# Token-major values in four column groups, and keys, queries and values of a pair's two head groups kept apart

## The chip, the cores and the metric

The kernel runs on one core of one Trainium2 chip. The metric is the device time of one execution in microseconds (us); lower is better. Engines are named as in the profile: PE is TensorE (matmuls; PEld its weight loads), DVE is VectorE, ACT is ScalarE, POOL is GpSimd, SP is SyncE, whose queue issues most DMA transfers.

## The reference, cut to what matters

The model has four layers, A, B, A, B, each with a residual around a LayerNorm. A is attention with a recurrent memory over 64 segments of 32 tokens; B is a mixer and an MLP over all 2048 tokens. All tensors are bf16, the width is 640, and A has 32 heads of 192.

```python
def _A_ref(x, mem0, Wq, Wk, Wv, Wo, seg_len):   # M = 8 memory rows, seg = 32
    mem = mem0
    for s in range(n_seg):
        h = jnp.concatenate([mem, x[:, s * seg:(s + 1) * seg]], axis=1)   # 40 rows
        q = jnp.einsum('btd,dhe->bhte', h, Wq)
        k = jnp.einsum('btd,dhe->bhte', h, Wk)
        v = jnp.einsum('btd,dhe->bhte', h, Wv)
        scores = jnp.where(mask, jnp.einsum('bhqe,bhke->bhqk', q, k) * scale, -1e9)
        o = jnp.einsum('bhqk,bhke->bhqe', _softmax(scores), v)
        o = jnp.einsum('bhte,hed->btd', o, Wo)
        mem = o[:, :M]
        outs.append(o[:, M:])

def _B_ref(x, w1, w2, w3, w4):
    h = _gelu(_layernorm(x) @ w1)
    # four quarters of h are shifted along the tokens by +1, -1, +2, -2
    x1 = x + shifted(h) @ w2
    return x1 + _gelu(_layernorm(x1) @ w3) @ w4
```

## The kernel before

Both attention layers run at once, as two lanes. Step `t` works on segment `t` of the first attention layer (lane 0) and on segment `t - 5` of the second (lane 1), so 69 steps do all the attention; steps 5 to 63 have both lanes, 80 rows (`NS`) in all, and the ten at the two ends have one lane, 40 rows (`L1`). Every second step a chunk of 64 tokens of each lane goes through layer B between the attention's matmuls.

The 32 heads are eight groups of four (`HG`), 768 weight columns each, and two groups make a pair; a step has four pairs. For each pair `proj_pair` (from L552) records the projections of both groups, and `attend` (from L658) records the rest of each group:

- Keys and queries (L577): 30 matmuls a group, 6 column blocks of 128 by 5 chunks of the contraction. The weight block is the stationary side and `hT`, the transposed rows, streams (80 columns; 56 in a one-lane step). The result, in PSUM as `psk` or `psq`, is copied to `kT` by three VectorE copies (L595, L601) and to `qT` by one ScalarE copy (L587).
- Values in a two-lane step: the same 30 matmuls into `psv`, a ScalarE copy to `vF` (L607), six transposes on TensorE into `pvt` (L615) and two copies to `V`, rows as tokens (L624 VectorE, L626 ScalarE).
- Values in a one-lane step (`values`, L630 on): the rows are the stationary side and 384 weight columns stream. The two groups of the pair lie in two column groups of 64 of the array (L641), so the result is token-major at once and is copied to `V` directly (L652, L654).
- `attend`: scores into `pss` (L670), minimum and mask on VectorE (L681), exponent to `Pm` on ScalarE (L688), sum, reciprocal and product on VectorE (L692 to L694), a transpose into `pst` (L703), a copy to `PT` (L708), the product with `V` into `pso` (L717), two copies to `oT` (L727, L729), and the output projection into `psy` (L744), which is shared by the whole step and whose first rows are the memory of the next step (L768 copies them to `hT`).

There is one `kT`, one `qT` and one `V`. `proj_pair` records both groups' projections first and then `attend` twice. So the copies of the second group land in the same tiles before the first group's scores and product read them: both groups of a pair compute with the keys, queries and values of the second.

The order on every engine is written by a planner (`Plan`). Each operation is added with an engine, an estimated duration and a due time. `place` then lays all operations out in time, on each engine taking among those that could start soonest the one with the earliest due time, and the kernel is written in that order. PSUM banks (six for attention, class A; two for layer B) and slots of the weight ring are given out in the course of it. Due times come from `AT` (shares of a pair's 12 us at which k, q and v are due) and `AT_J` (the same for the second group of the pair).

Weights do not all fit on the chip. Of each pair's key, query and value weights, some of the five chunks stay resident and the others (`STREAM`, `MORE`), 384 KB each, are loaded anew in every step by SP (L475) into a ring of nine slots (`RING_A`); layer B has a ring of three (L513). A slot is freed by the last matmul that reads it. A chunk holds the columns of both groups of the pair.

Of the kernel before, what the change touches and what calls it, by code (L numbers as in the profile page):

```python
# [27 lines left out]
V_ONE = (0, 1, 2, 3)  # L28
V_ON = ("DVE", "ACT")
KEEP = True  # L30
WO_FROM = 1
AT = (0.0, 0.2, 0.5)
AT_J = 0.1
# [6 lines left out]
OT_BUFS = 8  # L40
KT_BUFS = 1
VT_BUFS = 1
HALVES = tuple(range(8))
ONE = 56
WARM = (2, 4, 2, 1, 1, 1, 1, 6, 1, 1, 2, 1, 1)
LAT = 0.12
# [25 lines left out]
class Slotted(Buf):  # L72


    __slots__ = ("cls", "make", "slot", "left", "free_at", "obj")

    def __init__(self, cls, make):
        super().__init__()
        self.cls = cls
        self.make = make  # L80
        self.slot = None
        self.left = 0
        self.free_at = 0.0
        self.obj = None


class Op:
    __slots__ = ("e", "d", "due", "fn", "n", "succ", "ready", "slots", "start", "end", "dma", "i", "margin",
                 "paced", "last", "after")


class Plan:
# [8 lines left out]
    def add(self, e, d, due, fn, r=(), w=(), a=(), dma=0, queue=None, margin=0.0, after=()):  # L101
        op = Op()
        op.e, op.d, op.due, op.fn, op.dma, op.margin = e, d, due, fn, dma, margin
# [5 lines left out]
        preds = set(after)  # L109
# [31 lines left out]
    def place(self):  # L141
# [24 lines left out]
        srv = 0.0  # L166
        out = []

        def est(o, t):
            s = max(t, o.ready)  # L170
            need = {}
            for b in o.slots:
                if b.slot is None:
                    need[b.cls] = need.get(b.cls, 0) + 1
            for c, n in need.items():
                fs = self.free_slots[c]
                if len(fs) < n:
                    return None
                s = max(s, fs[n - 1][0])
# [14 lines left out]
        while left:  # L194
            best = None
            for e in engines:
# [17 lines left out]
                s, o = min((so for so in vals if so[0] <= lim), key=lambda so: (so[1].due, so[1].i))  # L214
# [9 lines left out]
            o.end = s + o.d  # L224
            free[e] = o.end
# [36 lines left out]
def kernel(  # L262
# [102 lines left out]
    vFw = ctile([P, GC * NS], bf16, "vF")  # L365
    vF = vFw[:].rearrange("p (c n) -> p c n", c=GC)
# [31 lines left out]
    nc.vector.memset(vFw[:], 0.0)  # L398
# [24 lines left out]
    def ps(cls, shape, dtype, name):  # L423
        b = Slotted(cls, None)

# [97 lines left out]
    kept = {}  # L523

# [11 lines left out]
    def attention_step(t):  # L536
# [17 lines left out]
        def proj_pair(i_, pr):  # L554
            s0 = base + sl * 2 * i_
            for kind, at in zip("kqv", AT):
                if i_ == 0 and t > 0 and KEEP:
                    wbs, wv = kept[kind]
                else:
                    wbs, wv = load_pair(kind, pr, s0 + at * 2 * sl, LEAD_A)  # L560
                if i_ == NPAIR - 1:
                    kept[kind] = wbs, wv
                if kind == "v" and not both and i_ in V_ONE:
                    values(i_, pr, s0 + at * 2 * sl, wbs, wv)
                    continue
                for j in range(2):
                    G = t * NG + 2 * i_ + j
                    due = s0 + (at + AT_J * j) * 2 * sl
                    pq = ps("A", [P, GC, NS], f32, "ps" + kind)

                    nres = KC - STREAM[kind] + MORE.get((kind, pr), 0)
                    for kcs in [range(0, nres)] + [range(kc, kc + 1) for kc in range(nres, KC)]:
                        def fn(op, pq=pq, wv=wv, j=j, kcs=kcs):
                            o = T(pq)
                            for cc in range(GC):
                                for kc in kcs:
                                    nc.tensor.matmul(out=o[:, cc, 0:W],  # L577
                                                     lhsT=wv(kc, GW * j + cc * P, GW * j + (cc + 1) * P),
                                                     rhs=h[:, kc, cw:cw + W], start=(kc == 0 and cc == 0),
                                                     stop=(kc == KC - 1), skip_group_check=True)  # L580
                        wb = wbs[0] if kcs[0] == 0 else wbs[1 + kcs[0] - nres]
                        add("PE", mm_us(W, k=GC * len(kcs)), due + 0.01 * kcs[0], fn, r=(wb, *hk), a=(pq,))
                    if kind == "q":
                        q = qT

                        def fq(op, pq=pq, q=q):
                            nc.scalar.copy(out=q[:, :, c0:c0 + N], in_=T(pq)[:, :, off:off + N])  # L587
                        add("ACT", act_us(GC * N), due, fq, r=(pq,), w=(B("qT"),))
                    elif kind == "k":
                        k_ = kT[G % KT_BUFS]  # L590

                        def fk(op, pq=pq, k_=k_):
                            p4 = T(pq)[:].rearrange("p (h c) n -> p h c n", h=2)
                            k4 = k_[:].rearrange("p (h c) n -> p h c n", h=2)
                            nc.vector.tensor_copy(out=k4[:, :, 0::3, c0:c0 + N], in_=p4[:, :, 0::2, off:off + N])  # L595
                        add("DVE", dve_us(4 * N), due, fk, r=(pq,), w=(B("kT", G % KT_BUFS, 0),))
                        for part, (r0, r1, jj) in enumerate(((0, 64, 1), (64, P, 2))):
                            def fk2(op, pq=pq, k_=k_, r0=r0, r1=r1, jj=jj):
                                p4 = T(pq)[:].rearrange("p (h c) n -> p h c n", h=2)
# [766 lines left out]
```

## Time and profile before

| | us |
|---|---|
| median of 3 runs | 3415.71 (3415.09 to 3416.42) |
| profiled execution, span from the first to the last instruction | 3411.3 |
| 0 to 90: the first step, weights arriving | PE busy 54 of 90 |
| 90 to 300: the other one-lane steps at the start | PE busy 194 of 210 |
| 300 to 3150: two-lane steps | PE busy 2817 of 2850 |
| 3150 to 3380: the one-lane steps at the end | PE busy 207 of 230 |
| 3380 to 3411: the last chunk of layer B | PE busy 20 of 31 |

The profile is of one execution; its span leaves out what lies before the first and after the last instruction. A busy TensorE is not one at its peak, since the ends of matmuls are modelled and their lengths overlap; how long a matmul occupies the engine is read from the distance of starts. The costliest groups that belong to the values, from the page (line, engine, operation, tiles, shape, count | busy us, mean ns | idle before, and what ended it):

```profile
L626 ACT COPY V<-pvt 80x384 bf16<-80x384 bf16 x472 | 224.2, 475 | 186.4 <-PE pvt L615 170.3
L607 ACT CAST vF<-psv 128x480 bf16<-128x480 f32 x472 | 262.2, 556 | 71.7 <-PE psv L577 66.7
```

### The profile page before, as it was taken

What the parts mean: (1) busy time and instruction counts of PE and PEld (TensorE: products, weight loads), DVE (VectorE), ACT (ScalarE), POOL (GpSimd) and SP (SyncE); (2) the same over time, 40 slices, a digit from 0 to 9 for tenths busy, and PEclk for the clock granted to TensorE, in tenths of its full rate; (3) what the DMA queues carried; (4) which work ended last, traced back from release to release, by engine and by line L of the source; (5) the groups of instructions that cost most, each with busy time, mean ns of one, the idle gap of its engine ahead of it and who ended that gap; (6) DMA issues with size and microseconds to landing.
All of it is one profiled execution on the core that took longest, in us unless ns stands there. A gap on an engine that the chain in (4) does not pass through costs nothing.

```text
span 3411.3 us, 183231 instructions
## 1 busy us (share of the span) xinstructions
PE 3293.4 (97%) x82493; PEld 3163.7 (93%) x82493; DVE 2395.2 (70%) x7360; ACT 1681.5 (49%) x4045; POOL 237.2 (7%) x488
## 2 busy tenths in 40 slices
PE   5989999999999999999999999999999999999987
PEld 4779999999999999999999999999999999999776
DVE  3667777777777777777667777767777777777665
ACT  1345545455555555555455555555555555555433
POOL 1000000000000000000000000000000000000000
PEclk7999999999999999999999999999999999999999
DMA  9777667766766776677668667766776676677775
GB/s 373 250 271 266 234 221 254 246 221 230 262 237 226 242 269 220 222 253 252 222 225 276 226 221 240 259 226 224 267 242 220 227 266 237 226 245 263 255 268 199
DMA packets 409739, 834.28 MB, mean 245 GB/s; under 512 B 39632, under 2 KB 207263, under 8 KB 408952
## 3 DMA queue, kind: packets, MB, share of 16 engines
q1 hardware_dynamic: 401656, 809.47, 69.3%
q8 instruction: 645, 10.57, 1.2%
q0 software_dynamic: 7136, 13.00, 1.1%
q14 instruction: 142, 1.16, 0.1%
q10 hardware_dynamic: 160, 0.08, 0.0%
HBM read 817.14 MB, written 5.24 MB: 241 GB/s over the span
## 4 chain that ended last, share of the span: by engine, by line
PE 91%; DMA 4%; issue 2%; DVE 1%; ACT 1%; SPq 1%; POOL 0%; POOLq 0%; ACTq 0%; DVEq 0%
PE psy L744 16%; PE psq L577 16%; PE psk L577 16%; PE psv L577 15%; PE pvt L615 5%; PE pso L717 4%; PE pss L670 4%; PE psh L1160 3%; PE y L1205 3%; PE pst L703 2%; PE psv L641 1%; PE psh L1038 1%; PE hs L1097 1%; DMA wst<-in_A_Wq_dram 1%; DMA wst<-in_A_Wv_dram 1%
## 5 line engine op out<-in xcount | busy, mean ns | idle before, releaser
L577 PEld LDWEIGHTS <-wst 128*128 128x128 bf16 x24468 | 994.5, 99 | 32.8 <-issue 18.0
L744 PE MATMUL psy<-oT,wo 128*128 128x80 bf16 (+1 forms) x16560 | 664.0, 200 | 14.1 <-DMA wo<-in_A_Wo_dram 7.4
L744 PEld LDWEIGHTS <-wo 128*128 128x128 bf16 x16560 | 616.0, 100 | 19.9 <-issue 10.3
L587 ACT CAST qT<-psq 128x480 bf16<-128x480 f32 (+1 forms) x552 | 292.2, 529 | 333.7 <-PE psq L577 323.9
L729 DVE CAST oT<-pso 128x240 bf16<-128x240 f32 (+1 forms) x552 | 214.5, 389 | 339.1 <-ACT oT L727 322.2
L577 PE MATMUL psk<-hT,wst 128*128 128x80 bf16 (+1 forms) x9108 | 430.1, 200 | 4.4 <-DMA wst<-in_A_Wk_dram 2.2
L577 PE MATMUL psq<-hT,wst 128*128 128x80 bf16 (+1 forms) x8280 | 401.1, 200 | 10.7 <-issue 6.5
L577 PE MATMUL psq<-hT,wq 128*128 128x80 bf16 (+1 forms) x8280 | 377.6, 200 | 14.6 <-DVE V L624 5.9
L688 ACT ACTIVATE Pm<-pss,sm 80x320 bf16<-80x320 f32 (+2 forms) x552 | 279.9, 507 | 200.4 <-DVE sm L681 200.2
L727 ACT CAST oT<-pso 128x240 bf16<-128x240 f32 (+1 forms) x552 | 190.2, 345 | 368.1 <-PE pso L717 343.6
L577 PE MATMUL psk<-hT,wk 128*128 128x80 bf16 (+1 forms) x7452 | 349.7, 200 | 16.9 <-ACT hT L768 10.8
L577 PE MATMUL psv<-hT,wst 128*128 128x80 bf16 x7080 | 348.3, 202 | 5.9 <-issue 5.5
L577 PEld LDWEIGHTS <-wq 128*128 128x128 bf16 x8280 | 328.0, 99 | 21.2 <-issue 14.3
L601 DVE CAST kT<-psk 64x160 bf16<-64x160 f32 (+1 forms) x1104 | 336.0, 304 | 14.6
L577 PE MATMUL psv<-hT,wv 128*128 128x80 bf16 x7080 | 332.7, 202 | 1.1 <-issue 0.8
L577 PEld LDWEIGHTS <-wk 128*128 128x128 bf16 x7452 | 299.5, 100 | 30.7 <-issue 29.2
L708 ACT COPY PT<-pst 80x320 bf16<-80x320 bf16 (+1 forms) x552 | 222.7, 403 | 209.1 <-PE pst L703 204.5
L626 ACT COPY V<-pvt 80x384 bf16<-80x384 bf16 x472 | 224.2, 475 | 186.4 <-PE pvt L615 170.3
L681 DVE CUSTOM_DVE_ANT_1 pss<-pss,mask 80x320 f32<-80x320 f32 (+2 forms) x552 | 251.7, 476 | 82.0 <-PE pss L670 79.0
L595 DVE CAST kT<-psk 128x320 bf16<-128x320 f32 (+1 forms) x552 | 254.8, 462 | 62.5 <-PE psk L577 55.0
L607 ACT CAST vF<-psv 128x480 bf16<-128x480 f32 x472 | 262.2, 556 | 71.7 <-PE psv L577 66.7
L577 PEld LDWEIGHTS <-wv 128*128 128x128 bf16 x7080 | 291.0, 100 | 6.1 <-issue 1.5
(146 smaller groups left out, 4646.0 us busy)
## 6 DMA issues: line engine op xcount, KB each, us to landing
wst<-in_A_Wk_dram SPq DMA_DIRECT2D x555, 384.0 KB, 5.2
wst<-in_A_Wq_dram SPq DMA_DIRECT2D x486, 384.0 KB, 5.2
wst<-in_A_Wv_dram SPq DMA_DIRECT2D x486, 384.0 KB, 5.3
wstB<-in_B_w_dram SPq DMA_DIRECT2D x495, 320.0 KB, 4.7
wstB<-in_B_w_dram SPq DMA_DIRECT2D x132, 160.0 KB, 4.6
wo<-in_A_Wo_dram SPq DMA_DIRECT2D x8, 960.0 KB, 12.5
xw<-in_A_x_dram POOLq DMA_DIRECT2D x31, 80.0 KB, 5.0
x2d<-vbg POOLq DMA_DIRECT2D x31, 80.0 KB, 5.0
```

The source lines that it names most:

```text
L577: nc.tensor.matmul(out=o[:, cc, 0:W], lhsT=wv(kc, GW * j + cc * P, GW * j + (cc + 1) * P), rhs=h[:, kc, cw:cw + W], start=(kc == 0 and cc ...
L587: nc.scalar.copy(out=q[:, :, c0:c0 + N], in_=T(pq)[:, :, off:off + N])
L595: nc.vector.tensor_copy(out=k4[:, :, 0::3, c0:c0 + N], in_=p4[:, :, 0::2, off:off + N])
L601: nc.vector.tensor_copy(out=k4[r0:r1, :, jj, c0:c0 + N], in_=p4[r0:r1, :, 1, off:off + N])
L607: nc.scalar.copy(out=vF[:, :, c0:c0 + N], in_=T(pq)[:, :, off:off + N])
L626: nc.scalar.copy(out=dst, in_=src)
L681: nc.vector.tensor_tensor_reduce(out=o, in0=o, in1=maskt.unsqueeze(1).to_broadcast([NR, HG, N]), scale=-scale, scalar=3.0e38, op0=ALU.add, ...
L688: nc.scalar.activation(out=Pb[0:NR, :, 0:N], in_=o, func=ACT.Exp, bias=sm_[0:NR, 0:1], scale=-1.0)
L708: nc.scalar.copy(out=Pt[:, :, 0:N], in_=T(pst)[0:NS, :, c0:c0 + N])
L727: nc.scalar.copy(out=o_[:, 3:6, off:off + N], in_=T(pso)[:, 3:6, 0:N])
L729: nc.vector.tensor_copy(out=o_[:, 0:3, off:off + N], in_=T(pso)[:, 0:3, 0:N])
L744: nc.tensor.matmul(out=o[:, m, cw:cw + W], lhsT=wo[:, cc, m * P:(m + 1) * P], rhs=o_[:, cc, 0:W], start=st, stop=True, skip_group_check=True)
```

## The change

1. `proj_pair` is split. `loads` gets the weights of a pair, `keys_queries` records the keys and queries of one group, and the values of both groups are recorded together. The recorded order of a pair is now: loads, keys and queries of the first group, values of both, `attend` of the first, keys and queries of the second, `attend` of the second. So the second group's copies to `kT` and `qT` wait until the first group's scores have read them. `V` has two tiles, one for each group of the pair.
2. In two-lane steps a new function, `values3`, replaces the value matmuls, the copy to `vF` and the transposes. The 80 rows are the stationary side, in three column groups of 32, 32 and 16; the fourth column group carries a quarter of the pair's columns for one of the three row parts. Three PSUM banks take 15 rounds of four matmuls of 384 columns, and six copies bring them to `V`.
3. The planner learns of the array's modes (`mode`, a price `SWITCH` for a change, and a preference to stay in a mode), of order edges (`order`) that add no wait of their own, and of banks kept free (`keep`: an operation of the keys or queries takes a bank only if two others stay free).
4. `AT`, `AT_J`, `OT_BUFS` and `VT_BUFS` change, and one LayerNorm step of layer B is recorded a little later.

```diff
-V_ONE = (0, 1, 2, 3)
-V_ON = ("DVE", "ACT")
+V_ONE = ("DVE", "ACT")
+V_ON = ("ACT", "DVE", "ACT", "ACT", "ACT", "DVE")
-AT = (0.0, 0.2, 0.5)
-AT_J = 0.1
+AT = (0.0, 0.1, 0.5)
+AT_J = 0.25
+KEEP_KQ = 2
-OT_BUFS = 8
+OT_BUFS = 7
-VT_BUFS = 1
+VT_BUFS = 2
+SWITCH = 0.095
...
-        preds = set(after)
+        preds = {*after, *order}
...
             for c, (k, n) in need.items():
                 fs = self.free_slots[c]
-                if len(fs) < n:
+                if len(fs) < n + k:
                     return None
...
-                s, o = min((so for so in vals if so[0] <= lim), key=lambda so: (so[1].due, so[1].i))
+                stay = e == "PE" and mode
+                s, o = min((so for so in vals if so[0] <= lim),
+                           key=lambda so: (so[1].mode != mode if stay else False, so[1].due, so[1].i))
...
-    vFw = ctile([P, GC * NS], bf16, "vF")
-    nc.vector.memset(vFw[:], 0.0)
...
+        def values3(i_, pr, s0, wbs, wv):
+            banks = [ps("A", [P, GWH], f32, "psv") for _ in range(3)]
+            for r in range(3):
+                def fv(op, r=r):
+                    o = T(banks[r])
+                    for kc in range(KC):
+                        for u in range(4):
+                            g3, b = (u, r) if u < 3 else (r, 3)
+                            n3 = min(32, NS - 32 * g3)
+                            a = GWH * b
+                            nc.tensor.matmul(out=o[32 * u:32 * u + n3, :], lhsT=h[:, kc, 32 * g3:32 * g3 + n3],
+                                             rhs=wv(kc, a, a + GWH), start=(kc == 0), stop=(kc == KC - 1))
+                add("PE", mm_us(GWH, k=KC), s0 if r == 0 else s0 - STEP + 0.01 * r, fv, r=(*wbs, *hk),
+                    w=tuple(banks) if r == 0 else (), a=(banks[r],) if r else (), mode=32, order=placed_before("pso") if r == 0 else ())
+            for r in range(3):
+                v_copy(V_ON[r], s0, banks[r], (0, NS), (r // 2, r % 2, 0, NS), B("V", r // 2, r % 2, 0))
+                n3 = min(32, NS - 32 * r)
+                v_copy(V_ON[3 + r], s0 + 0.1, banks[r], (96, 96 + n3), (1, 1, 32 * r, 32 * r + n3), B("V", 1, 1, r))
...
-            add("PE", mm_us(N, N, 4) + mm_us(2 * N, N, 2), hi - HI[0], fs,
-                r=(B("qT"), B("kT", G % KT_BUFS, 0), B("kT", G % KT_BUFS, 1), B("kT", G % KT_BUFS, 2)), w=(pss,))
+            last_op["pss"] = add("PE", mm_us(N, N, 4) + mm_us(2 * N, N, 2), hi - HI[0], fs,
+                order=placed_before("pst"), r=(B("qT"), B("kT", G % KT_BUFS, 0), B("kT", G % KT_BUFS, 1), B("kT", G % KT_BUFS, 2)), w=(pss,))
...
-            proj_pair(i_, pr)
+            got = loads(i_, pr)
+            keys_queries(i_, pr, 0, got)
+            (values3 if both else values)(i_, pr, base + sl * 2 * i_ + AT[2] * 2 * sl, *got["v"])
             attend(2 * i_, 2 * pr)
+            keys_queries(i_, pr, 1, got)
             attend(2 * i_ + 1, 2 * pr + 1)
```

`v_copy` copies one bank's rows to one `V` tile, on the engine that `V_ON` (two lanes) or `V_ONE` (one lane) names. `pst` has an order edge after the last `pso`, like that of `pss` after the last `pst`. The matmuls of `keys_queries`, of `values` and of `attend` are those of before.

## The prediction

> **What bounds the kernel now.** I read the page's engine line, the chain that ended last, the idle time in windows, TensorE's timeline in two places, then the waits of SP's DMA queue and the DMA issues.
>
> ```profile
> span 3411.3 us, 183231 instructions
> ...
> PE 3293.4 (97%) x82493; PEld 3163.7 (93%) x82493; DVE 2395.2 (70%) x7360; ACT 1681.5 (49%) x4045; POOL 237.2 (7%) x488
> ...
> PE 91%; DMA 4%; issue 2%; DVE 1%; ACT 1%; SPq 1%; POOL 0%; POOLq 0%; ACTq 0%; DVEq 0%
> ```
> ```profile
> 2000.00:3150.00 1150.00, 1138.95 (x28569) 1115.81 (x28566) 832.13 (x2494) 598.07 (x1397) 77.61 (x157) 1.00 0.71 241
> 3150.00:3380.00 230.00, 207.11 (x5545) 176.75 (x5542) 152.71 (x547) 92.97 (x268) 17.07 (x35) 0.99 0.76 265
> ```
>
> TensorE is the bound: 97% busy, 91% of the chain, and in the two-lane steps (the first window) idle for 11 of 1150 us. So a TensorE instruction saved there is time saved. The one-lane steps at the end are looser: 207 of 230 us.
>
> A two-lane step pays for a pair's values so (start, length, engine, line, tiles, count):
>
> ```profile
> 1002.77 0.60 PE L577 MATMUL psv<-hT,wv 128*128 128x80 bf16 x12
> 1003.20 0.81 PE L577 MATMUL psv<-hT,wst 128*128 128x80 bf16 x18
> 1003.85 0.73 PE L670 MATMUL pss<-kT,qT 128*128 128x80 bf16 x12
> 1004.42 0.59 PE L577 MATMUL psv<-hT,wv 128*128 128x80 bf16 x12
> 1004.85 0.50 PE L615 MATMUL pvt<-ident,vF 128*128 128x128 bf16 x6
> 1005.18 0.81 PE L577 MATMUL psv<-hT,wst 128*128 128x80 bf16 x18
> ```
>
> Lengths overlap, so take starts: the 30 matmuls of one group run from 1002.77 to 1003.85, 36 ns each; six transposes from 1004.85 to 1005.18, 56 ns each. The new form has one relative in the trace, the one-lane L641, which uses two column groups of 64:
>
> ```profile
> 3204.82 0.54 PE L670 MATMUL pss<-kT,qT 128*128 128x40 bf16 x12
> 3205.30 0.51 PE L641 MATMUL psv<-wv,hT 128*40 128x384 bf16 x4
> 3205.64 0.65 PE L641 MATMUL psv<-wst,hT 128*40 128x384 bf16 x6
> 3206.22 0.37 PE L717 MATMUL pso<-PT,V 80*128 80x40 bf16 x8
> ```
>
> Ten matmuls of 384 columns take 3205.30 to 3206.22, 0.92 us. Their single records start 3 ns apart in twos, and the twos 163 ns apart: both column groups stream at once, and a round costs one stream of 384 columns (the 128-column transpose at 56 ns gives 0.42 ns a column, 160 ns, and 3 over). Entering the mode costs 80 ns (the first start follows its forerunner by 109 to 130 ns where 25 to 40 is usual), leaving it 95 ns (258 where 163 is usual).
>
> **The change, part by part.**
>
> *Values in 59 two-lane steps, 4 pairs each, 236 pairs.* Removed per pair: 60 x 36 ns + 12 x 56 ns = 2.832 us. Added: 60 matmuls in four column groups of 32, 15 rounds of four. If four groups share a round as two do: 15 x 163 + 80 + 95 = 2.620 us; in the new order all 60 stand together, so one entry and one exit. Saved 0.212 us x 236 = **50.0 us**. Bounds of the round: 163 ns, if the 3 ns are a price of each stream; 170 ns, if each further group adds 3.3 ns (15 x 236 x 7 = 25 us less saved); 326 ns, if the groups went two by two. I take 163, the row itself; the last is a rival.
>
> A rule speaks against it. The Trainium skill, "TensorE: Matmul & The Clock Gate", Part 3 (what overlaps and what doesn't), lets a weight load overlap a running matmul only where the row group differs; column groups share all rows. The trace disagrees for two groups: L641's weight loads last 95 to 100 ns, start within 3 ns of the matmuls that run, and the round is still 163. By the rule each of the 3540 rounds would be some 100 ns longer, an estimate of 354 us more.
>
> *One-lane steps.* The two value blocks of a pair now stand together: the new order enters the 64-column mode 40 times instead of 72. 32 x 175 ns = **5.6 us** saved.
>
> *Copies.* Per pair ScalarE had 2 x (556 + 475) ns and gets 4 x 475 = 1.90 us; VectorE had 2 x 350 and gets 2 x 552 (L652, the same 384 f32 columns), 94 us more in all: 2395 becomes 2490, under 75%. Hidden under TensorE's 97%. Without that cover it would be the 0.4 us a pair.
>
> *Waits among the engines.* Each TensorE wait has a cover: the TensorE work, priced at its rows, that stands between the instruction that starts a chain and the one that waits for its end. I counted covers in both built orders and compared them with what the chains take in this trace. Gone: the waits of psq for V's copies (L624) and of pvt for vF, 11.4 and 3.2 us in the steady part by the starts of the records. New: the second group's keys and queries may be copied to kT and qT only after the first group's scores. Queued behind such a waiting copy are VectorE's softmax and ScalarE's exponents, and the chain's next link, pst, waits for these. Scores to pst need 3.0 us (2.76 from the trace, 0.2 for the last matmul's end and the release); a tenth of the new covers is under 3.10, and the sum short is 2.5 us (before 1.7). pst over PT to pso needs 0.73 us (0.51 likewise); the tenth falls from 0.86 to 0.71, and 7.1 us are short where none were. oT and qT: 5.3 us, before 1.9. Where the two old waits stood, pst and pso are what is late next. So 11 us more by count, 15 less: **0**, with -15 and +25 as ends (the kept wait for hT at each step's head, some 20 us, stays).
>
> *Weight chunks.* The nine-slot ring is the tight place, as SP's queue shows (whom it waited for, us in all, times, longest; then one kind of chunk with its median us from issue to landing):
>
> ```profile
> SPq L475 <- PE psk L577: 747.9, 288, 17.6
> SPq L475 <- PE psv L577: 225.2, 219, 3.7
> ```
> ```profile
> wst<-in_A_Wk_dram SPq DMA_DIRECT2D x555, 384.0 KB, 5.2
> ```
>
> SP issues a chunk when PE has freed its slot. A key or query chunk serves both groups of a pair, and the second group's matmuls now come after the first's scores, so the slot is freed later. From the freeing matmul to the first use of the new chunk, two-lane steps, the cover falls from a median of 9.6 us to 8.1, its least value from 6.0 to 3.8. Needed, from the freeing matmul's issue to landing: a median of 5.15 us, 5.65 in the worst quarter. Short of 5.15: 6.5 us in the two-lane part, 9.2 and 4.9 in the first and last one-lane steps, before 0.2 in all: **+20**. Ends: 0 (a late chunk's wait lengthens its neighbours' cover) and +74 (short of 5.65: 53.8 + 15.4 + 13.0, before 8.3).
>
> *The rest.* A vF memset goes and one for a second V comes: under the first step's loads, under 1 us if bare. One LayerNorm step of the MLP is recorded later, 0.45 us on VectorE: order alone. The order edges issue nothing. Of the moved second group, 60 matmuls, three kT copies and one qT copy, all are counted above; its loads aren't moved, since a pair's chunks are still loaded at once, but q's fall due 1.2 us earlier in SP's queue (0.1 for 0.2 of 12 us), ahead of the MLP's chunks; POOL's queue is not passed. Seven oT for eight: a step's eighth group takes the first's, whose psy stands early. All **0**.
>
> Sum: 3411.3 - 50.0 - 5.6 + 0 + 20 = 3376 us of span. The median of the runs shown, 3415.7, is 4.4 us above the profiled span; with these **3380 us**.
>
> **The rivals.** (A) *The ring decides.* Place: L475's issues behind psk and psq. Price +74 instead of +20: 3434 us. It decides from landings of about 5.5 us, where the shortfall eats the 55.6 us saved. For it: 69% DMA busy already, bursts of three chunks, SP's 748 us behind psk. Against: a median landing leaves 20. (B) *Four column groups don't share a round.* Each ns of a round costs 3.54 us, so from 10 ns more (35 us) the change loses; two by two, 3380 + 577 = 3957 us. For it: no row has four. Against: two cost what one does. The skill's same part lists 2.38x for three column groups; by that ratio, an estimate, a round would be some 26% longer, 150 us in all. (C) *The ring costs nothing*, because waits overlap: 3360 us, and 3345 if also the 15 us of removed waits come without new ones. (D) *Nothing measurable*: the saved 55.6 us go into short covers, as (A) at 49 to 63 us of its price. That the change doesn't do what it says is excluded for the order (per group psk, psq, pss; 14160 matmuls of 32 columns), so this is no case.
>
> **How the numbers follow.** My forecast, 3362 to 3408: 0.48. (C), under 3362: 0.18. (D), within 0.2% (7 us, about what a measurement of this kernel can tell from no change): 0.09. (A): 0.15. (B): 0.10. Faster 0.66, same 0.09, slower 0.25. The range runs from 3350, short of (C)'s end, to 3440, just past (A); above it lies most of (B) and a little of (A). The forecast's own range is 3362 to 3402.
>
> **What would show it.** Right: psv rounds of four with starts 163 ns apart, pvt gone from the chain, two two-lane steps taking about 97.5 us where 98.9 stood, PE still 96 to 97%, psk and psq waiting for wst some 10 to 20 us. Wrong: rounds of 172 ns or more, weight loads of psv with idle time before them, DMA above 5% of the chain, or pst waiting for Pm over 20 us.

## The result, and the profile after

The changed kernel takes 3433.97 us (median of four executions, 3425.65 to 3441.15); the kernel before, run beside it, 3415.4. The ratio is **1.0053, with a 95% interval of 1.0036 to 1.0069**: some 18 us slower, where 3380 us and a gain of 36 were forecast. The profiled execution is the lowest of the four. The page's span, engine line and chain:

```profile
span 3424.0 us, 177449 instructions
...
PE 3268.9 (95%) x79659; PEld 2858.7 (83%) x79661; DVE 2495.6 (73%) x7360; ACT 1678.2 (49%) x4045; POOL 240.1 (7%) x487
...
PE 70%; DVE 15%; ACT 5%; DMA 5%; issue 3%; SPq 1%; POOL 0%; POOLq 0%; DVEq 0%; ACTq 0%
```

The chain has changed hands: TensorE fell from 91% to 70%, VectorE rose from 1% to 15%, ScalarE from 1% to 5%. VectorE is only 73% busy. The two stretches shown of before, in the answer by windows (start:end, length, busy us of PE, PEld, DVE, ACT and POOL, clock, DMA share, GB/s):

```profile
2000.00:3150.00 1150.00, 1130.11 (x27482) 994.62 (x27480) 871.23 (x2495) 596.57 (x1399) 77.79 (x156) 1.00 0.71 241
3150.00:3380.00 230.00, 201.45 (x5279) 172.60 (x5276) 148.88 (x532) 87.72 (x257) 18.47 (x37) 0.98 0.72 253
```

In the two-lane window TensorE idles for 20 of 1150 us, where 11 stood. The new value block in TensorE's timeline (start, length, line, tiles, shape, count):

```profile
2004.13 0.60 PE L591 MATMUL psq<-hT,wst 128*128 128x80 bf16 x12
2004.65 0.67 PE L636 MATMUL psv<-wv,hT 128*32 128x384 bf16 x12
2005.15 0.50 PE L636 MATMUL psv<-wst,hT 128*32 128x384 bf16 x8
2005.48 0.66 PE L636 MATMUL psv<-wv,hT 128*32 128x384 bf16 x12
2005.96 0.50 PE L636 MATMUL psv<-wst,hT 128*32 128x384 bf16 x8
2006.29 0.66 PE L636 MATMUL psv<-wv,hT 128*32 128x384 bf16 x12
2006.78 0.50 PE L636 MATMUL psv<-wst,hT 128*32 128x384 bf16 x8
2007.21 0.32 PE L708 MATMUL pst<-ident,Pm 80*128 80x80 bf16 x4
```

Sixty matmuls take 2004.65 to 2007.21, 2.56 us. Single records start within 10 ns of each other in fours, and nearly all of the fours 162 to 163 ns apart (one in a block 172 to 174). With an entry 95 ns dearer than the usual distance of starts a pair costs 2.65 us, against 2.62 forecast. So most of the work was saved: 2.83 − 2.65 = 0.18 us a pair, 43 us for 236 pairs, where 50.0 were forecast. With every TensorE instruction priced at its row, the whole kernel holds 3212.7 us before and 3158.2 after, 54.5 less (forecast 50.0 + 5.6). That is some 6 us more than 43 + 5.6, so some 6 us of the value blocks' own time stand among the stalls counted next.

What was lost are waits. I compared every distance of TensorE's starts with the price of the row; what is over is a stall:

| stretch (steps) | length before | after | stalls before | after |
|---|---|---|---|---|
| first step | 88.9 | 89.5 | 54.1 | 55.4 |
| 1 to 4, one lane | 166.1 | 173.5 | 27.6 | 37.2 |
| 5 to 60, two lanes | 2768.9 | 2758.7 | 71.7 | 105.6 |
| 61 to 63, two lanes | 146.5 | 152.3 | 3.2 | 11.3 |
| 64 to 67, one lane | 171.4 | 177.8 | 27.1 | 35.9 |
| end, to the last matmul | 65.1 | 67.8 | 19.6 | 23.0 |

By what they waited for, the new stalls of steps 5 to 60 are: pst for VectorE's product `Pm` 24.7 us (1.6 before), layer B's transposes for `vbg` 12.2, pso for `PT` 6.7, pss for `kT` 5.6. Gone are psq for V (10.2) and pvt for vF (3.2). In lengths: 43 us of work were saved, and steps 5 to 63 became 10.2 − 5.8 = 4.4 us shorter, so some 39 us of new waits lie there. The answer on waits has the same (engine, tile and line, whom it waited for, us in all, times, longest), first before:

```profile
ACT Pm L688 <- DVE sm L681: 200.2, 204, 2.9
...
PE pst L703 <- DVE Pm L694: 8.5, 13, 1.6
```

and after:

```profile
ACT Pm L693 <- DVE sm L686: 318.3, 317, 1.8
...
PEld L708 <- DVE Pm L699: 34.0, 64, 2.2
...
PE pst L708 <- DVE Pm L699: 25.4, 62, 2.1
...
PEld L819 <- DVE vbg L811: 22.7, 36, 6.9
```

So ScalarE's exponent waits 318.3 us for the minimum where 200.2 stood, and pst 25.4 us for `Pm` where 8.5 stood (steps 5 to 60 alone: 24.7 for 1.6). One such place, by the timeline of all engines (in brackets the idle time before, and what ended it):

```profile
1584.82 0.55 DVE L623 CAST V<-psv 80x384 bf16<-80x384 f32 x1 [0.66 <-PE psv L636]
...
1585.41 0.97 ACT L623 CAST V<-psv 32x384 bf16<-32x384 f32 x2 [0.43 <-DVE V L623]
...
1585.67 0.45 PE L675 MATMUL pss<-kT,qT 128*128 128x80 bf16 x6
...
1586.41 0.56 DVE L623 CAST V<-psv 16x384 bf16<-16x384 f32 x1 [1.04 <-ACT V L623]
...
1587.01 0.49 DVE L686 CUSTOM_DVE_ANT_1 pss<-pss,mask 80x320 f32<-80x320 f32 x1
...
1587.64 0.52 ACT L693 ACTIVATE Pm<-pss,sm 80x320 bf16<-80x320 f32 x1 [0.93 <-DVE sm L686]
...
1588.92 0.49 DVE L699 TENSOR_TENSOR Pm<-Pm,sm 80x320 bf16<-80x320 bf16 x1
...
1589.46 0.32 PE L708 MATMUL pst<-ident,Pm 80*128 80x80 bf16 x4 [0.36 <-DVE Pm L699]
```

The scores' last record ends at 1586.12, but the minimum (L686) starts at 1587.01. Ahead of it in VectorE's queue stands the last copy to `V`, of 16 rows, and that idles for 1.04 us until a ScalarE copy is done, the second of the two in ScalarE's line, which takes 80 other rows out of the same PSUM bank. By the order of the copies, all 95.5 us for which VectorE's V copies wait for ScalarE's are waits for a copy of the same bank: copies of one bank overlap in none of the 236 pairs, while copies into the same `V` tile from two banks do overlap, 120 times each in e7 and e14 below. So it is the shared bank that keeps them apart, not the tile that they write. From the scores' start to pst 3.79 us pass; the forecast had 3.0. TensorE stands still behind it. An engine may be idle, as VectorE is here for 1.04 us, and yet hold the chain: the minimum starts only when the copy recorded ahead of it is done.

### The profile page after: what moved, and what is told of

It reads as the page before. It is cut to its first block, busy times and chain, and to the rows that moved or that the text cites. A ratio compares the mean times of both kernels' runs of the same rounds, so it can differ in the third digit from the quotient of the medians.

```text
span 3424.0 us, 177449 instructions
## 1 busy us (share of the span) xinstructions
PE 3268.9 (95%) x79659; PEld 2858.7 (83%) x79661; DVE 2495.6 (73%) x7360; ACT 1678.2 (49%) x4045; POOL 240.1 (7%) x487
## 4 chain that ended last, share of the span: by engine, by line
PE 70%; DVE 15%; ACT 5%; DMA 5%; issue 3%; SPq 1%; POOL 0%; POOLq 0%; DVEq 0%; ACTq 0%
PE psq L591 14%; PE psk L591 14%; PE psv L636 12%; PE psy L749 11%; PE pso L722 4%; PE psh L1167 3%; PE pss L675 3%; DMA wst<-in_A_Wq_dram 3%; ACT V L623 2%; PE pst L708 2%; DVE V L623 2%; PE y L1212 2%; DVE Pm L699 2%; DVE sm L697 2%; DVE pss L686 2%
## 5 line engine op out<-in xcount | busy, mean ns | idle before, releaser
L591 PEld LDWEIGHTS <-wst 128*128 128x128 bf16 x17388 | 702.8, 99 | 28.4 <-issue 10.0
L749 PE MATMUL psy<-oT,wo 128*128 128x80 bf16 (+1 forms) x16560 | 672.7, 200 | 29.4 <-DVE oT L734 8.0
L749 PEld LDWEIGHTS <-wo 128*128 128x128 bf16 x16560 | 619.6, 100 | 35.6 <-issue 26.1
L623 ACT CAST V<-psv 80x384 bf16<-80x384 f32 (+2 forms) x1024 | 485.5, 474 | 274.9 <-PE psv L636 163.4
L636 PEld LDWEIGHTS <-hT 128*32 128x32 bf16 (+1 forms) x14160 | 351.3, 94 | 204.0 <-issue 17.5
L591 PE MATMUL psk<-hT,wst 128*128 128x80 bf16 (+1 forms) x9108 | 444.6, 200 | 5.9 <-issue 4.6
L693 ACT ACTIVATE Pm<-pss,sm 80x320 bf16<-80x320 f32 (+2 forms) x552 | 279.1, 506 | 320.8 <-DVE sm L686 318.3
L623 DVE CAST V<-psv 16x384 bf16<-16x384 f32 (+2 forms) x552 | 307.1, 556 | 161.3 <-ACT V L623 95.5
L636 PE MATMUL psv<-wv,hT 128*32 128x384 bf16 (+1 forms) x7080 | 415.1, 327 | 0.4 <-issue 0.2
L636 PE MATMUL psv<-wst,hT 128*32 128x384 bf16 (+1 forms) x7080 | 412.2, 326 | 0.0
L686 DVE CUSTOM_DVE_ANT_1 pss<-pss,mask 80x320 f32<-80x320 f32 (+2 forms) x552 | 258.7, 469 | 111.3 <-PE pss L675 100.1
L591 PEld LDWEIGHTS <-wk 128*128 128x128 bf16 x7452 | 307.4, 99 | 29.5 <-issue 23.9
```

The lines of the kernel that those rows point to most:

```text
L591: nc.tensor.matmul(out=o[:, cc, 0:W], lhsT=wv(kc, GW * j + cc * P, GW * j + (cc + 1) * P), rhs=h[:, kc, cw:cw + W], start=(kc == 0 and cc ...
L623: (nc.vector.tensor_copy if e == "DVE" else nc.scalar.copy)(out=v_part(*dst), in_=a_)
L636: nc.tensor.matmul(out=o[32 * u:32 * u + n3, :], lhsT=h[:, kc, 32 * g3:32 * g3 + n3], rhs=wv(kc, a, a + GWH), start=(kc == 0), stop=(kc == ...
L686: nc.vector.tensor_tensor_reduce(out=o, in0=o, in1=maskt.unsqueeze(1).to_broadcast([NR, HG, N]), scale=-scale, scalar=3.0e38, op0=ALU.add, ...
L693: nc.scalar.activation(out=Pb[0:NR, :, 0:N], in_=o, func=ACT.Exp, bias=sm_[0:NR, 0:1], scale=-1.0)
L749: nc.tensor.matmul(out=o[:, m, cw:cw + W], lhsT=wo[:, cc, m * P:(m + 1) * P], rhs=o_[:, cc, 0:W], start=st, stop=True, skip_group_check=True)
```

## The experiments

My theory before them was that the short covers of these chains take the gain, fed by the V copies; the main rival was the forecast's own (A), the weight ring. Ratios are to the kernel before on the same chip; 0.001 is 3.4 us. The planner writes a new order for nearly every edit, so the cleanest runs are those that change the size of an instruction and leave all in its place ("same order" below).

### Is it the ring?

**e1** and **e5**: every streamed key, query and value chunk loads only the first group's 768 columns, and the second group reads these too, in the kernel after (e1) and in the kernel before (e5); same order.

```diff
-                nc.sync.dma_start(out=T(b)[:, 0:PW], in_=w_src[kind][:, kc, cols])
+                nc.sync.dma_start(out=T(b)[:, 0:GW], in_=w_src[kind][:, kc, PW * pr:PW * pr + GW])
-            return T(slots[kc - nres])[:, c0:c1]
+            return T(slots[kc - nres])[:, c0 % GW:c0 % GW + c1 - c0]
```

> The changed kernel with every instruction in its place, but each streamed chunk of key, query and value weights brings only the first group's 768 columns, 192 KB for 384, and the second group reads these too (so the second group's streamed share of the products is left out). Ring theory (chunks land late because their slots are freed later): the changed kernel's excess over its TensorE work is mostly landings, so the time falls by 25 us or more, to 3395-3410, and the runs draw together. Waits theory (chains of VectorE and ScalarE between TensorE's instructions give back what the values save): within 10 us of the changed kernel, 3420-3440; the one-lane steps alone become some us shorter. Serial theory (one kT and one qT make a group wait for the other, and the last group's chain lies bare at a step's end): as the waits theory.

> The control of the half loads: the kernel before with the same edit (192 KB for each streamed chunk of keys, queries and values; the second group reads the first's columns, so its streamed share is left out), every instruction in its place. The changed kernel fell by 76 us with it. Ring theory (late chunks are the change's own loss): before falls by 25-45 us, most of it in the one-lane steps, to 3375-3395, and the changed kernel with half loads (3358) is the faster of the two by 20 us or more. Waits theory: before falls by 65 us or more, to 3345-3355, so that the change stays about as far behind without late chunks as with them.

Measured: e1 3357.76 us, ratio 0.982 (0.9805 to 0.9835); e5 3342.82, 0.9778 (0.9752 to 0.9804). Halving the loads saves 0.0233 after and 0.0222 before, some 80 and 76 us: the same within the intervals. With half loads, where TensorE waits for no chunk in steps 5 to 60, the change still costs 0.0042, some 14 us. In e1 pst still waits 26.7 us for `Pm`, and the chains of e1 and of e5 differ as those of after and before did:

```profile
PE 73%; DVE 16%; ACT 6%; issue 3%; DMA 1%; SPq 0%; POOL 0%; POOLq 0%; DVEq 0%; ACTq 0%
```
```profile
PE 95%; DVE 1%; ACT 1%; issue 1%; SPq 0%; DMA 0%; POOL 0%; POOLq 0%; ACTq 0%; DVEq 0%
```

**e6**: a tenth slot, paid for with four `oT` instead of seven.

```diff
-RING_A = 9
-OT_BUFS = 7
+RING_A = 10
+OT_BUFS = 4
```

> The changed kernel with ten ring slots for nine; oT has four tiles for seven to make room, which alone moves no instruction. Covers of streamed chunks rise (the tenth part from 5.9 to 6.3 us in the two-lane steps, the median from 8.7 to 10.3; from 5.4 to 5.6 or 5.7 in the one-lane steps). Ring theory: 20-40 us less than the changed kernel, 3395-3415, with the one-lane steps shorter by some 15 us in all. Waits theory: 3425-3435, the waits of pst for Pm and of layer B's transposes for vbg as they were.

Measured: 3458.53 us, 1.0122 (1.0093 to 1.0152). A larger ring, and slower than after by 0.0069, some 24 us, outside both expected ranges: pst for `Pm` 31.7 us, and psy for `oT` 29.5 as a new wait. With four `oT` and a new order this is no clean test of the ring; the pair e1 and e5 is, and by it the ring as the cause falls.

### Which part of the change?

**e3**: the new values with the old recorded order and old due times. **e4**: the new order with the old values path (and six `oT`). **e16**: after with the old due times alone. **e8**: layer B's LayerNorm step recorded at its old place.

```diff
+            for kind in "kq":                       # e3: order of before
+                for j in range(2):
+                    keys_queries(i_, pr, j, got, kind)
...
-            (values3 if both else values)(...)      # e4: values2 is the path of before
+            (values2 if both else values)(...)
...
-AT = (0.0, 0.1, 0.5)                                # e16, and in e3
-AT_J = 0.25
+AT = (0.0, 0.2, 0.5)
+AT_J = 0.1
...
+        if not last:                                # e8: ahead of the first transposes
+            add("DVE", 0.45, D(0.08), f3, ...)
```

> The values in four column groups alone: keys of both groups, queries of both, then values, then both attends, with the old due times, so both groups again use the second's keys and queries (the first group's own are left out), while V has a tile for each. Serial theory: the waits came with the order, so nearly all of the saved 50 us shows: 3360-3380. Waits theory (V copies in the queues): the waits stay, 3395-3415. Ring theory: the slots are freed early again, 3365-3385.

> The new order alone: groups one after the other with the old value matmuls, copy to vF and transposes, in the place of the new values (oT has six tiles for seven, since vF takes the room). Serial theory: TensorE's work is that of before plus a few us, and the order's waits are paid in full, 3460-3490. Waits theory (V copies are to blame): 3415-3440. Ring theory: 3450-3480, with psk and psq waiting for chunks.

> The kernel after with the old due times alone (queries at 0.2 instead of 0.1 of a pair, the second group 0.1 instead of 0.25 of a pair later), recorded order as in after. Theory 'the new due times are part of what keeps the chain covered': the second group's keys and queries come up before the first group's scores have released kT and qT, stalls rise, 3450 to 3600. Rival 'the due times brought the new waits': 3400 to 3425 with pst waiting for Pm under 10 us.

> The changed kernel with the one LayerNorm step of layer B recorded where it was before, ahead of the transposes of vb. Waits theory: the wait of these transposes for vbg (12 us in the two-lane steps, some 4 in the others) stays or moves to the next VectorE product, since VectorE's queue decides: within 10 us of the changed kernel, 3424-3444. If the moved step is to blame the time falls by 12-20 us, to 3414-3422. Ring theory: no change.

Measured: e3 3767.22 us, 1.1018 (1.0997 to 1.1039), with pst waiting 106.5 us for `Pm` and pso 80.2 for `PT` in steps 5 to 60. e4 3563.21, 1.0419 (1.0404 to 1.0435): psy waits some 65 us for `oT`, pso 34 for `PT`. e16 3662.52, 1.0719 (1.0696 to 1.0743): layer B's matmuls alone wait 67.8 us for VectorE's `hTB`. e8 3447.69, 1.0085 (1.0057 to 1.0113): the transposes' wait for `vbg` doubles, 12.2 to 26.1 us. e3 and e4 lie far above every expected range, e16 above the 3600 of its theory, e8 4 us above the range of its waits theory, with an interval that overlaps after's. Each is a new order to which the due times weren't fitted, so these runs price no part. They show that the parts don't add: the values with the old order and due times lose, and so does the new order with the old values or the old due times. In all four the largest new stalls are waits of TensorE for VectorE and ScalarE.

### The V copies

Same order as after in all of these. **e2**: the copies of two-lane values to `V` move 8 of 192 columns per head. **e9**: only VectorE's two of the six. **e10**: only ScalarE's four. **e11**: e1 and e2 together. The other columns of V are not written in two-lane steps.

```diff
-                a_ = T(bank)[src[0]:src[1], :].rearrange("n (a b) -> n a b", a=2)
-                (nc.vector.tensor_copy if e == "DVE" else nc.scalar.copy)(out=v_part(*dst), in_=a_)
+                n_ = 8 if e == "DVE" and both else Dh    # e9; "ACT" in e10
+                a_ = T(bank)[src[0]:src[1], :].rearrange("n (a b) -> n a b", a=2)[:, :, 0:n_]
+                (nc.vector.tensor_copy if e == "DVE" else nc.scalar.copy)(out=v_part(*dst)[:, :, 0:n_], in_=a_)
```

> The changed kernel with every instruction in its place, but each copy of values from PSUM to V moves 16 of 384 columns a row (the rest of V is left as zeros). Waits theory in the form that the V copies stand in VectorE's and ScalarE's queues ahead of the softmax: the waits of pst for Pm and of layer B's transposes for vbg, 25 and 12 us in the two-lane steps, fall under 10 together and the time falls by 25 to 40 us, to 3390-3410. Serial theory: those waits come from kT, qT and the chain itself; the time falls by less than 12 us. Ring theory: no change beyond 5 us.

> The changed kernel with every instruction in its place; in two-lane steps only VectorE's two V copies of a pair are cut to 16 of 384 columns a row (the rest of these parts of V is zeros), ScalarE's four are whole. The run that cut all six fell by 31 us. VectorE theory (these copies stand ahead of the softmax of the same pair in VectorE's queue): 3395-3415, and the waits of pst for Pm in the two-lane steps fall from 25 us to under 5. ScalarE theory (PT and the exponents wait behind its four copies): 3425-3440.

> The mirror image: ScalarE's four V copies of a pair are cut to 16 of 384 columns a row, VectorE's two are whole, every instruction in its place. VectorE theory: 3422-3438, pst's waits for Pm still over 15 us. ScalarE theory: 3395-3415.

> Both cuts at once in the changed kernel, in the same order: half of each streamed chunk and 16 of 384 columns of every V copy. Half loads alone gave 3358, the kernel before with half loads 3343. VectorE theory: with late chunks gone, what the V copies' waits held back shows in full; the two-lane steps lose 30 us or more against the half loads alone: 3315-3330, below before with half loads. Serial theory (one kT and one qT): 3345-3358, since the order's waits stay.

| | us | ratio | 95% interval | two-lane steps 5 to 60, us |
|---|---|---|---|---|
| after | 3433.97 | 1.0053 | 1.0036 to 1.0069 | 2758.7 |
| e2, all six short | 3402.94 | 0.9944 | 0.9922 to 0.9966 | 2747.9 |
| e9, VectorE's short | 3407.66 | 0.9949 | 0.9929 to 0.9968 | 2746.5 |
| e10, ScalarE's short | 3413.63 | 0.998 | 0.996 to 1.0 | 2748.0 |
| e1, half loads | 3357.76 | 0.982 | 0.9805 to 0.9835 | 2744.8 |
| e11, half loads and all six short | 3316.64 | 0.9685 | 0.9666 to 0.9705 | 2713.6 |

e10 was a miss for the theory that VectorE's own copies are what costs: ScalarE's are worth nearly as much. The place shown above explains both, since the chain runs through ScalarE's copies, then VectorE's, then the minimum. The same place in e9 (its lines are one further down):

```profile
1580.82 1.08 ACT L624 CAST V<-psv 32x384 bf16<-32x384 f32 x2
...
1581.46 0.45 PE L676 MATMUL pss<-kT,qT 128*128 128x80 bf16 x6
...
1581.93 0.18 DVE L624 CAST V<-psv 16x16 bf16<-16x16 f32 x1 [1.15 <-ACT V L624]
1582.14 0.49 DVE L687 CUSTOM_DVE_ANT_1 pss<-pss,mask 80x320 f32<-80x320 f32 x1
...
1584.05 0.49 DVE L700 TENSOR_TENSOR Pm<-Pm,sm 80x320 bf16<-80x320 bf16 x1
...
1584.73 0.31 PE L709 MATMUL pst<-ident,Pm 80*128 80x80 bf16 x4
```

The copy takes 0.18 us for 0.56, the minimum starts 0.68 us after the scores' start instead of 1.34, and pst comes without a wait, 3.27 us after them. In e10 it is 0.76 and 3.27. In steps 5 to 60 the wait of pst for `Pm` falls from 24.7 us to 0.2 (e2), 0.4 (e9) and 0.7 (e10). With late chunks present (e2, e9, e10) part of what is freed goes to them: TensorE's waits for DMA in steps 5 to 60 rise from 4.1 us to 13.0 to 16.6, mostly psq, and the stalls end at 94 to 96 us. Without late chunks (e11) the cut is worth 0.0135 instead of 0.0109, and steps 5 to 60 take 2713.6 us, where the kernel before with half loads (e5) takes 2748.5: 35 of the 50 us that the values were to save in all two-lane steps. So the V copies that stand ahead of the minimum hold pst's wait for `Pm`, some 24 of the 39 us of new waits. `vbg`'s 12.2 us stay in e2, e9, e10 and e11: another chain, whose cause isn't shown. Nor was the same cut made in the kernel before, where TensorE waits 13.4 us for copies to V and vF in steps 5 to 60; so how much of e2's 37 us is the change's own isn't shown, and the 35 us compare a kernel with short copies to one with whole ones.

### A version that beats both

**e7**: e6 with one V copy of the six on VectorE, the third. **e14**: that edit without the tenth slot, with the first copy, not the third, on VectorE. **e15**: e7 with the one-lane steps recorded as in e13 below.

```diff
-RING_A = 9                                          # e7 and e15
-OT_BUFS = 7
-V_ON = ("ACT", "DVE", "ACT", "ACT", "ACT", "DVE")
+RING_A = 10
+OT_BUFS = 4
+V_ON = ("ACT", "ACT", "DVE", "ACT", "ACT", "ACT")   # e14: ("DVE", "ACT", ...), nine slots, seven oT
```

> Ten slots as in the run before, and of a pair's six V copies only one on VectorE for two (the third bank's rows; ScalarE has five). Waits theory (V copies stand in VectorE's queue ahead of the softmax): pst's waits for Pm fall by half or more, and the time is 10-25 us under that with ten slots alone. Ring theory: the same as with ten slots alone, within 8 us. Serial theory: the same, with pss waiting for kT.

> The kernel after, nine slots and seven oT as they are, with only the first of the six V copies on VectorE and five on ScalarE. Theory 'V copies on VectorE': the placement alone, without the tenth slot, takes out most of what e7 took out of e6 (62 us), so 3372 to 3400 and pst waiting for Pm under 8 us. Rival 'the tenth slot is needed': at nine slots the freed time is taken up by late chunks as in e2 and e9, 3405 to 3425 with 10 us or more of TensorE waits for DMA. Rival 'any new plan is a lottery': above 3430.

> e7 (ten slots, four oT, one V copy of the six on VectorE; 3396 us) with the one-lane steps recorded as in e13. If the one-lane recording costs 22 us and adds up with the rest: 3374 (3366 to 3384). If e13's rival holds: 3388 to 3404, as e7.

Measured: e7 3396.15 us, **0.9937 (0.9919 to 0.9954)**, 0.0185 or some 63 us under e6, with pst's wait for `Pm` at 0.3 us in steps 5 to 60. e15 3389.18, **0.991 (0.9892 to 0.9929)**, the lowest with whole loads and whole copies, though its interval overlaps e7's: within its rival's range, and not the 3374 of its theory. In its ten one-lane steps both groups of a pair use the second's keys and queries, as in the kernel before; e7 keeps the groups apart everywhere. e15's chain is TensorE's again:

```profile
PE 92%; DMA 3%; issue 2%; ACT 1%; DVE 1%; SPq 1%; POOL 0%; POOLq 0%; ACTq 0%
```

e14 missed: 3446.37, 1.0083 (1.0064 to 1.0101), no faster than after (1.0036 to 1.0069). Its chain has VectorE at 2%, as e7's, but DMA at 8%; in steps 5 to 60 stalls are 128.1 us, of them 16.2 for DMA, and psy waits some 30 us for copies to `oT` (after: 3):

```profile
PE 86%; DMA 8%; issue 2%; DVE 2%; ACT 1%; SPq 1%; POOL 0%; POOLq 0%; DVEq 0%; ACTq 0%
```

e14's time is in the range of its rival 'any new plan is a lottery'. So one V copy on VectorE freed the softmax chain in all three orders, but what comes of it hangs on the order that the planner writes, and part of e7's gain may be luck with it. The tenth slot with four `oT` alone (e6) is slower than after, and the placement alone (e14) at least no faster; as e14 also has another copy on VectorE than e7, and more `oT`, what makes e7 pay wasn't separated.

### The one-lane steps

Steps 1 to 4, 61 to 67 and the end take 22.3 us more than before (table above), with half loads too (e1 over e5: 5.5, 4.4, 11.0 and 1.8). **e12** puts the recorded order of keys and queries back in the ten one-lane steps; **e13** the due times, kept banks and order edges too; **e18** also the price of the value blocks, without a mode; **e17** also one V tile. TensorE's order at the two ends is then near before's, but not the same: it differs around layer B's chunks.

```diff
+            for kind in "kq":                                            # e12, if not both
+                for j in range(2):
+                    keys_queries(i_, pr, j, got, kind)
...
-            for kind, at in zip("kqv", AT):                              # e13
+            for kind, at in zip("kqv", AT if both else AT_ONE):          # (0.0, 0.2, 0.5)
-                pq = ps("A", [P, GC, NS], f32, "ps" + kind, KEEP_KQ)
+                pq = ps("A", [P, GC, NS], f32, "ps" + kind, KEEP_KQ if both else 0)
...
-                add("PE", mm_us(GWH, k=KC), ..., mode=64)                # e18
+                add("PE", mm_us(GWH, k=KC) + 0.15, ...)
...
-            k_, V_ = kT[G % KT_BUFS], Vt[p_ % 2]                         # e17
+            k_, V_ = kT[G % KT_BUFS], Vt[p_ % 2 if both else 0]
```

> The changed kernel with the old recorded order (keys of both groups, queries of both, values, both attends) in the ten one-lane steps alone, where both groups thus use the second's keys and queries again (the first group's own are left out); the two-lane steps keep the new order. Serial theory: the one-lane steps 1 to 4 and 64 to 67 fall from 173 and 178 us to about 166 and 171 as before, 12-20 us in all: 3410-3424. If late chunks or the lost eighth oT explain these steps instead, they stay within 4 us: 3428-3440.

> The kernel after with everything that the change altered in the recording of the ten one-lane steps put back: the recorded order (both groups' keys, then queries), the old due times (0, 0.2, 0.5 and 0.1 for the second group), no banks kept free, no order edges. The two-lane steps are recorded as in after. Theory 'one-lane recording': these are what made steps 1-4, 61-67 and the end 22 us longer (7.4 + 5.8 + 6.4 + 2.8), so they come back to within 2 us each of before (166, 147, 171, 75) and the time is 3412 (3404 to 3420). Rival 'not the recording': the one-lane steps are longer because of what stays (values of both groups in one block, two V tiles, the LayerNorm step, the neighbouring two-lane steps, seven oT), the stretches stay at 173, 152, 178, 78 and the time within 3425 to 3444.

> e13 with the two edits of the one-lane steps that it had left: their value blocks get no mode (0.15 us of estimate as before, so the planner no longer keeps the two blocks of a pair together) and both groups of a pair use one V tile there (so in these ten steps the first group's product reads the second group's values). TensorE's order at the two ends is then that of before. Theory 'one-lane recording': steps 1-4 and 64-67 come back to within 3 us of before (166 and 171) and the time is 6 to 20 us under e13. Rival 'what the steps are next to' (seven oT, the LayerNorm step, queues of the two-lane steps beyond the joint, the granted clock): 172 to 178 and 176 to 181 as in after, and the time within 7 us of e13 (3429).

> e17 with the two V tiles kept in the one-lane steps, so that only the mode's edit is added to e13. If the planner's wish to stay in the 64-column mode is what lengthened the one-lane steps, this is as e17; if the two V tiles are (the product of the second group no longer waits for the first's), it is as e13, 3429.

| | us | ratio | 95% interval | 1 to 4 | 61 to 63 | 64 to 67 | end |
|---|---|---|---|---|---|---|---|
| before | 3415.4 | 1 | | 166.1 | 146.5 | 171.4 | 65.1 |
| after | 3433.97 | 1.0053 | 1.0036 to 1.0069 | 173.5 | 152.3 | 177.8 | 67.8 |
| e12 | 3444.03 | 1.0056 | 1.0034 to 1.0077 | 180.1 | 150.8 | 179.2 | 67.9 |
| e13 | 3429.17 | 1.0027 | 1.0014 to 1.004 | 174.3 | 150.0 | 179.1 | 65.1 |
| e18 | 3427.12 | 1.001 | 0.9997 to 1.0023 | 173.3 | 151.0 | 179.3 | 66.1 |
| e17 | 3427.35 | 1.0017 | 1.0004 to 1.0031 | 173.6 | 148.5 | 176.3 | 65.8 |

The four together, which the recording was to bring back to 549.1 us, stay at 564 to 578; e12's time lies above both of its ranges, and e17 and e18 can't be told apart. By ratio e13, e17 and e18 are 9 to 15 us better than after, a gain that one profiled execution of each doesn't place. So the recording costs at most a part, and the steps are still 15 us longer in e17. Its trace says where: matched piece by piece with before's, its steps 1 to 4 fall behind by 7.5 us, 5.0 of them in the two stretches where layer B's transposes and what follows stand in another order (before's 131 to 160 and 221 to 246 us). What else e17 has of the change, seven `oT`, the LayerNorm step of layer B and the queues past the joint, is left; e17 with that step at its old place wasn't run, and e8, which has it there, keeps the new recording (175.1 us in steps 1 to 4). The granted clock of steps 1 to 4 varies from 0.95 (e13) to 0.99 (after), an estimate of some 7 us in itself, so single profiles don't settle it. This part stays open. Steps 61 to 63 are another matter: they have both lanes, and with short V copies take 147 to 149 us (e2, e9, e10).

## Why the prediction was wrong

- **Values, −50.0: right in kind, 7 us too much.** Four column groups share a round as two do; rival (B) falls. But a pair took 2.65 us against 2.62, 0.03 us x 236 = 7: entering the mode cost 95 ns, not 80 (the forecast's own rows, by the distance usual for each forerunner, give mostly 84 to 94), and the 15 rounds 14 ns more than 15 x 163. The forecast's 0.42 ns a column doesn't follow from the one row it names (56 ns over 128 columns are 0.44, 168 ns a round); its 163 was taken from the row of rounds, so nothing hangs on it.
- **Waits among the engines, 0: this step failed.** In the two-lane steps stalls rose by 33.9 + 8.1 = 42 us, some 6 of them the value blocks' own time: some 36 us of waits by this count and 39 by the lengths, past the +25 that was the upper end. (The lengths include waits for DMA.) The largest is pst for `Pm`, 24.7 us where 1.6 stood. The count took the old trace's 3.0 us for scores to pst. In the new queues a V copy that itself waits stands ahead of the minimum, and the same chain takes 3.79 us. e2, e9, e10 and e11 show it: shorten the copies on either engine, leave all else in place, and this wait goes. The rest (`vbg` 12.2, `PT` 6.7, `kT` 5.6) stays for the most part in them, and its cause is open.
- **Copies, hidden under TensorE's 97%: the wrong cover.** Counting 94 us of VectorE's busy time against its idle time said nothing of where in the queue the copies stand. The six follow one value block (in the timeline shown first they run from 2005.70 to 2009.14, behind a block that starts at 2004.65), where before one on each engine followed each group. The forecast listed what waits behind the copies to `kT` and `qT`, and left out the copies to `V`.
- **Weight chunks, +20: too much, and no cause.** Waits for DMA rose by some 3 to 6 us over the whole kernel, as one counts them. Half loads bring some 76 to 80 us in both kernels (e1, e5). The price of rival (A), 3434 us, is the measured time to a microsecond, by another mechanism. That is luck: a time that fits is no proof. The ring matters as the next limit; it takes part of what a freed chain gives (e2, e9, e10).
- **Mode changes, −5.6, in the one-lane steps: outweighed.** These steps and their neighbours lost 22 us in the profile; why stays open.
- **The sum.** Forecast span 3376, profiled 3424.0, 48 us apart. The two-lane steps were to gain 50 and pay 6.5 for the ring, 43.5 net; they gained 4.4, so 39 us of the miss lie there, 7 of them the values and the rest the waits. The rest were to lose 14.1 − 5.6 = 8.5 and lost 17.1, so 9 more. The median then lies 10 us over the profiled span instead of 4.4.
- **The signs that it named.** Rounds of 163 ns came; pst waiting for `Pm` over 20 us, named as a sign against it, came too; two two-lane steps took 98.5 us, not 97.5, and TensorE was 95% busy, not 96 to 97.

## What to carry to other kernels

When the bound engine loses work, its helpers' chains lose cover: count each chain again with the new queue order, and for every instruction that waits ask what latency chain is queued behind it, however idle its engine is. A block that does in one go what was done in two delivers its evacuation copies in one burst; look for a place for that burst where no chain starts, and give the copies of one PSUM bank to one engine, so that none waits for the other's (neither was tried here). To price a suspect, shrink that one instruction with the order kept, and run the same cut on the kernel before as a control, as was done here for the loads and not for the copies.

## What the runs showed of the hardware

Four column groups of at most 32 columns stream together: 162 to 163 ns a round, as for two groups of 64, and the weight loads (85 to 97 ns) stay hidden in all 236 blocks, 227 of which take 2.553 to 2.556 us. The Trainium skill, "TensorE: Matmul & The Clock Gate", Part 3 (the mechanism), lets loads overlap running matmuls only where the row group differs; these runs show loads hidden that differ in the column group alone. The full-array matmuls of the kernel before speak against that sentence too: L577's loads last 99 to 100 ns, and its matmuls start 36 ns apart.

Half-size chunks bring 76 us in the kernel before, whose TensorE is 97% busy: much of it in the first step (88.9 to 76.3 us) and the one-lane steps (166.1 to 152.9 and 171.4 to 153.3), where the rows are few and the weights the same.
